# Conv taps at other rounds and in other homes, and a first step whose end is shared with GpSimd, in a convolution and GELU kernel

## The chip, the cores and the metric

One core of one Trainium2 chip. The metric is the device time of one execution in microseconds; the median of three runs stands for a kernel. Engines are named as the profile names them: PE (TensorE), ACT (ScalarE), DVE (VectorE), POOL (GpSimd), SP (SyncE, which only issues DMAs).

## What is computed

x has 8 x 4096 tokens of 192 features. Each feature group of 24 (8 heads) has 7 causal taps; the conv is a weighted sum of the last 7 tokens, with weights from a softmax. Its result goes through two matrix products with a GELU between them:

```python
w = softmax(weight)                       # (8 heads, 7 taps)
out = np.einsum('hk,bskhg->bshg', w, x_unf)   # depthwise causal conv
h = out.reshape(B * S, D) @ w_in          # 192 -> 2048
g = h * (1.0 / (1.0 + np.exp(-1.702 * h)))
return (g @ w_out)                        # 2048 -> 192
```

All of it is float32.

## The kernel before

**Tiles and steps.** The tokens are worked in 32 steps of 1024 (two batch halves n of 512 tokens, as 2 x 256 columns). Features lie on partitions, 64 of them at a time, in three chunks c. `w_in_s` holds 12 blocks of w_in and 9 places for sums of blocks; `conv_t` holds the conv result of one step in six own blocks (0 to 5) and their *common sums* (6 to 19: a sum or a difference of two blocks); each block lies there twice, the second time with its partition halves exchanged ("crossed"). `g` holds the GELU results. `slots` (three pairs of PSUM banks) and `sums` (one pair) are the accumulators.

**Step 0** (`first_step`) loads and rounds the weights while it computes, and does its second product in `second_first`, a generator that is stepped through between the stages. Its last part, up to L1020, forms in this order: the common sums of step 1 (`make_common_1`, L631: 9 sums on DVE, crossings on ACT by L603, one by SP's DMA), the late sums 16 to 19 (`make_late_1`), the sums of w_in (`sums_w_in`, 21 for column half v = 1, then 25 for v = 0, all on DVE, L435 to L443), the sums 13 to 15 (`make_rest_1`), and four transposes `turn` (L1025) that put the four quarters of the result into `osbs`, whence `store` (L1036) writes them out over SP's queue. The products of this part run through four half banks; the last one, `c21`, stays in a bank of `slots[1]` until its transpose has read it. Meanwhile `add_forms` (L480 on ACT, L482 on POOL) makes sums of w_out by copies and accumulating DMAs, and the first *taps* of step 2 are made. `load_x(3)` (L99, SP) is the last thing that `first_step` issues.

**Steps 1 to 31** have two halves. `hidden` runs the list `HIDDEN`, an order written out by hand: 41 *terms* (`mm`, L710; one product of a sum of w_in with a sum of the conv, in a Strassen-like scheme; the first is fetched at the end of the step before), copies of accumulators on ACT or DVE (`copy`, L801 and L803, into `KS`, the places k0 to k8), joins on DVE (L814), GELUs on ACT (L820, L827). `second` runs the list `PLAN` in the same way for the second product (L1107). Each term's operand pair (block of w_in, block of conv) stands in `TERMS[v][t]`; term `(0, 8)` of v = 0 is the first in `HIDDEN`, `(0, 14)`, which needs common sum 14, the nineteenth. `copy a k8`, which writes spot 1, stands ahead of the eighteenth, `join o2` and `gelu 0` near it. `HIDDEN` also holds `turn` (L518: transposes of x two steps on), `over`, `ve` and `vc` (common sums of the next step on POOL, and crossings on SP, L601).

**Taps.** The conv of the step after next is made in 21 taps (3 chunks x 7). In most of them ACT multiplies the shifted x by the weight of a tap (L567) into a *home*, some part of `g`, `osbs` or `room` that is free for a while (`TAP_SPOTS`, `TAP_HALVES`, `first_taps`; `spot(i)` names a place of 4 x 256 columns, spots 0 and 1 are `osbs`, where results wait for their store). The home is then added into `conv_t` by POOL (chunk 2, L569) or, pairwise in a tree, by accumulating DMAs of POOL's queue (`LATER`, L587; in steps up to 2 `TREE`, L592). `("tap",)` in the lists marks where one is made. Step 2 is an exception: chunks 0 and 2 by taps, chunk 1 by DVE, the tree of chunk 0 ending with `(3, 5)` and `(0, 3)`, which `end_taps` issues at the end of `first_step`.

**What orders the work.** Each engine's queue, SP's and POOL's too, runs in the order in which the program issues; waits come from the tiles that are read and written. A DMA's issue counts as an instruction of its queue and waits there for its operands.

Of the kernel before, what the change touches and what calls it, by code (L numbers as in the profile page):

```python
# [15 lines left out]
def kernel(  # L16
# [142 lines left out]
    TAP_HALVES = {1: ((1, 0), (1, 2), (11, 0), (2, 0), (2, 2), (11, 2)), 2: ((11, 2), (13, 0), (11, 2), (13, 2), (11, 2), (13, 0)), 3: ((12, 2), (16, 2), (15, 2), (16, 0), (15, 0), (12, 0))}  # L159
# [273 lines left out]
    def add_up(v, dst, a, op, b, eng=vec):  # L433
        if op == "+":
            eng.tensor_add(v(dst), v(a), v(b))  # L435
        elif op == "-":
            eng.tensor_sub(v(dst), v(a), v(b))  # L437
        elif op == "n":
            vec.scalar_tensor_tensor(
                out=v(dst), in0=v(a), scalar=-1.0, in1=v(b), op0=ALU.mult, op1=ALU.subtract  # L440
            )
        else:
            vec.tensor_scalar_mul(v(dst), v(a), -1.0)  # L443
# [81 lines left out]
    first_taps = [row(0, 6), row(0, 7)] + [spot(i)[:, k : k + 2, :] for i in (13, 18) for k in (0, 2)]  # L525
# [17 lines left out]
    def conv(big, c, k, ns=slice(0, 2), times=vec.tensor_scalar_mul):  # L543
# [99 lines left out]

    def make_rest_1():
        for item in SUMS_ES:
            sum_of(1, item, vec)
        for r in (V_S, V_E):
            if r[1] > r[0]:
                cross_run(1, *r, act.copy)
# [32 lines left out]
    def prepare(big):  # L682

        def convs(*cs):
            for c in cs:
                for k in range(K):
                    yield "", 0.76 if k else 0.48, lambda c=c, k=k: conv(big, c, k)

        if big < 3:
            yield from convs(1)  # L690
# [42 lines left out]
    def plain(u, m, n, v, slot, ks=range(NC), first=0):  # L733
# [40 lines left out]
    def hidden(big, tiles, work):  # L774
# [19 lines left out]
        def copy(eng, dst, src, sign):  # L794
# [4 lines left out]
            for out, i in pairs:  # L799
# [4 lines left out]
                else:  # L804
                    vec.tensor_scalar_mul(out, i, -1.0)

# [23 lines left out]

        def turn():
            if big + 2 < N_BIG:
                c = next(turns)
                if c == 0:
                    need(f"done {big + 1}")
                transpose_x(big + 2, c)
                if c == NC - 1 and big + 3 < N_BIG:
# [572 lines left out]
```

## Time and profile before

| | us |
|---|---|
| median of 3 runs (2325.21 to 2330.69) | 2327.47 |
| the profiled execution's own time | 2326.97 |
| its span, first to last instruction | 2325.2 |
| PE busy | 2291.7 |
| DVE, ACT, POOL busy | 2161.8, 1701.8, 1093.8 |

The granted TensorE clock is 0.994 on average. In rows of the timeline the first number is the start in us from the span's begin, the second the length, then engine, line, operation, tiles written and read, and the count of merged instructions; in brackets stands the idle time of the engine before them and what ended it. In rows of groups there stand the count, the busy time in us, the mean length in ns, and the idle time before with its releasers; in rows of DMA issues the count, the size and the median us from issue to landing. In a table of windows each engine's busy us are followed by the granted clock, the share of the DMA engines and GB/s. Matmul rows show fewer records than instructions in places; starts are reliable, ends are modelled.

### The profile page before, as it was taken

The numbers are of one execution on the slowest core, as the hardware profiler recorded it, in microseconds if no ns is written. First come the engines' busy times: TensorE is split into PE (matmuls) and PEld (weight loads), VectorE is DVE, ScalarE is ACT, GpSimd is POOL, SyncE is SP. The second block draws the span as 40 slices with busy tenths as digits, with TensorE's granted clock in tenths as the row PEclk, the third lists the DMA queues.
The fourth block names the chain that finished last, engine by engine and source line by source line (L and its number), as shares of the span: only waits on it lengthen the run. The fifth ranks groups of instructions, "written<-read, shape, count | busy, mean of one in ns | idle before, by whom it ended". The sixth has DMA issues, their size and how long they took to land.

```text
span 2325.2 us, 64148 instructions
## 1 busy us (share of the span) xinstructions
PE 2291.7 (99%) x25090; PEld 1321.8 (57%) x25090; DVE 2161.8 (93%) x3059; ACT 1701.8 (73%) x3338; POOL 1093.8 (47%) x1218
## 2 busy tenths in 40 slices
PE   9899999999999999999999999999999999999999
PEld 5265555555555755555655555555555555555555
DVE  8899999999999998999899899999999999999998
ACT  8677777777777777777677677777777777777745
POOL 1444554444554445544455444555444554454610
PEclk9899999999999999999999999999999999999999
DMA  9967789777797777987788877889877889776743
GB/s 202 155 126 153 152 167 177 152 153 155 144 180 156 153 151 149 174 166 147 141 158 167 165 154 153 159 154 176 161 155 151 159 163 175 156 153 132 150 98 69
DMA packets 347917, 358.12 MB, mean 154 GB/s; under 512 B 131424, under 2 KB 268896, under 8 KB 347616
## 3 DMA queue, kind: packets, MB, share of 16 engines
q0 software_dynamic: 82192, 196.32, 48.2%
q1 hardware_dynamic: 263776, 157.32, 29.8%
q8 instruction: 199, 3.26, 0.6%
q14 instruction: 102, 0.84, 0.1%
q10 hardware_dynamic: 1648, 0.39, 0.1%
HBM read 53.15 MB, written 25.17 MB: 34 GB/s over the span
## 4 chain that ended last, share of the span: by engine, by line
PE 88%; DVE 6%; DMA 2%; issue 2%; ACT 1%; POOL 1%; SPq 0%; DVEq 0%; ACTq 0%; POOLq 0%
PE slot L710 35%; PE slot L1107 26%; PE sums L1107 15%; PE sums L710 12%; DVE room L435 1%; DVE g L437 1%; DVE room L437 1%; DMA g<-in_moe_w_in_dram 0%; DMA room<-g 0%; DMA g<-osbs 0%; DVE osbs L1025 0%; DMA conv_t<-conv_t 0%; SPq L340 0%; POOL g L437 0%; DVE w_out_s L420 0%
## 5 line engine op out<-in xcount | busy, mean ns | idle before, releaser
L710 PE MATMUL slot<-conv_t,w_in_s 64*128 64x512 f32 x3372 | 931.3, 594 | 9.7 <-DVE osbs L1025 6.6
L1107 PE MATMUL slot<-g,w_form 128*32 128x256 f32 x5872 | 727.8, 380 | 0.1
L710 PEld LDWEIGHTS slot<-conv_t,w_in_s 64*128 64x128 f32 x3372 | 441.7, 188 | 342.5 <-issue 266.1
L437 DVE TENSOR_TENSOR g<-g 128x1024 f32<-128x1024 f32 x372 | 445.8, 1225 | 16.6 <-ACT g L827 9.2
L1107 PEld LDWEIGHTS slot<-g,w_form 128*32 128x32 f32 x5872 | 367.7, 110 | 121.4 <-ACT room L1132 11.6
L1107 PE MATMUL sums<-g,w_form 128*32 128x256 f32 x3800 | 427.6, 379 | 0.0
L710 PE MATMUL sums<-conv_t,w_in_s 64*128 64x512 f32 x1284 | 425.5, 593 | 0.3 <-DVE w_in_s L420 0.3
L437 POOL TENSOR_TENSOR conv_t<-conv_t 128x256 f32<-128x256 f32 x300 | 267.1, 963 | 223.6 <-PE slot L710 82.5
L820 ACT ACTIVATE g<-slot 128x512 f32<-128x512 f32 x494 | 265.1, 626 | 127.7 <-PE slot L710 127.2
L567 ACT ACTIVATE g<-xt,cw 128x512 f32<-128x512 f32 x418 | 289.6, 726 | 71.4 <-DVE g L437 44.7
L1107 PE MATMUL slot<-g,w_out_s 128*32 128x256 f32 x4080 | 324.0, 381 | 4.0 <-DVE room L435 3.8
L1083 POOL DMA_DIRECT2D g<-g x124 | 118.3, 954 | 436.7 <-PE slot L1107 236.8
L569 POOL TENSOR_TENSOR conv_t<-conv_t,g 128x512 f32<-128x512 f32 x180 | 293.7, 1632 | 52.1 <-ACT g L567 49.5
L1132 ACT COPY room<-slot 32x256 f32<-32x256 f32 x434 | 158.2, 365 | 202.0 <-PE slot L1107 189.4
L1107 PEld LDWEIGHTS sums<-g,w_form 128*32 128x32 f32 x3800 | 219.2, 110 | 79.5 <-ACT room L1132 5.7
L710 PEld LDWEIGHTS sums<-conv_t,w_in_s 64*128 64x128 f32 x1284 | 179.2, 187 | 123.9 <-issue 99.7
L1107 PEld LDWEIGHTS slot<-g,w_out_s 128*32 128x32 f32 x4080 | 162.8, 110 | 92.0 <-ACT g L820 11.4
L710 PE MATMUL slot<-g,w_in_s 64*128 64x512 f32 x556 | 205.2, 596 | 6.9 <-ACT room L801 6.5
L827 ACT ACTIVATE g<-g 128x1024 f32<-128x1024 f32 x155 | 170.9, 1102 | 0.4 <-DVE g L814 0.4
L1132 ACT COPY room<-sums 32x256 f32<-32x256 f32 x217 | 79.0, 364 | 94.0 <-PE sums L1107 83.1
L1107 PE MATMUL slot<-osbs,w_form 128*32 128x256 f32 x1240 | 147.2, 381 | 0.4 <-ACT slot L1136 0.3
L820 ACT ACTIVATE g<-sums 128x512 f32<-128x512 f32 x188 | 104.0, 616 | 58.7 <-PE sums L710 56.8
(241 smaller groups left out, 4029.3 us busy)
## 6 DMA issues: line engine op xcount, KB each, us to landing
g<-g POOLq DMA_DIRECT2D x124, 512.0 KB, 6.6
xin<-in_x_dram SPq DMA_DIRECT2D x240, 180.0 KB, 6.4
conv_t<-conv_t SPq DMA_DIRECT2D x662, 64.0 KB, 2.0
g<-g POOLq DMA_DIRECT2D x120, 256.0 KB, 6.4
out_dram<-osbs SPq DMA_DIRECT2D x186, 128.0 KB, 4.5
conv_t<-g POOLq DMA_DIRECT2D x89, 256.0 KB, 4.4
g<-g SPq DMA_DIRECT2D x248, 64.0 KB, 3.9
g<-room POOLq DMA_DIRECT2D x31, 512.0 KB, 5.5
```

The costliest lines, as they stand in the source:

```text
L435: eng.tensor_add(v(dst), v(a), v(b))
L437: eng.tensor_sub(v(dst), v(a), v(b))
L567: act.mul(home, conv_src(big, c, k), cw[:, c, k : k + 1])
L569: nc.gpsimd.tensor_add(dst, dst, home)
L710: nc.tensor.matmul(slot[h], w_in_s[halves[h], a, v * P : (v + 1) * P], src, start=first, stop=True, skip_group_check=True,)
L820: act.activation(dst[:, :, h, :], ot(bank(src, h)), AF.Gelu_apprx_sigmoid, scale=float(sign))
L827: act.activation(dst.rearrange("p o h t -> p h o t"), src, AF.Gelu_apprx_sigmoid, scale=float(sign))
L1083: nc.gpsimd.dma_start(out=spot(dst), in_=spot(a), accum_op=ALU.add)
L1107: nc.tensor.matmul(dst, w, t, start=first, stop=last, skip_group_check=True)
L1132: act.copy(to, d)
```

## The change

In the regular steps: one of the two taps at the start of `HIDDEN` goes, one is added near the end of `PLAN`, one near its start is added and a later one taken out (the first three taps come one place earlier); `TAP_HALVES` gives other homes to chunks 1 and 2, and two entries of `LATER` name other partners.

At step 0's end: the nine common sums and the 25 sums of w_in's half 0 go to POOL, the first ahead of everything else that POOL does from there on; an `n` sum is two instructions there. The crossings of 6 to 11 go from ACT to SP. Sum 13 is made by DVE before the last products, sums 14 and 15 by POOL behind ten taps (before: eight), with their crossing on SP. Two transposes of the result come between the last products; `c21` is copied by ACT to a place `last` in `room`, and the two other transposes and both stores move into step 1, behind the first two `copy v` (two parts). In step 1 the other taps, the convs of chunk 1, `turn`, `over`, `ve` and `vc` come later, by a list `count`. `first_taps` and `TAP_HALVES[3]` name other homes for step 2's taps: spot 18, which is also k6, is no longer one; spots 5 and 6 are.

```diff
-    TAP_HALVES = {1: ((1, 0), (1, 2), (11, 0), (2, 0), (2, 2), (11, 2)), 2: ((11, 2), (13, 0), (11, 2), (13, 2), (11, 2), (13, 0)), 3: ((12, 2), (16, 2), (15, 2), (16, 0), (15, 0), (12, 0))}
+    TAP_HALVES = {1: ((3, 0), (1, 0), (11, 0), (2, 0), (2, 2), (11, 2)), 2: ((11, 2), (13, 0), (16, 2), (15, 2), (11, 2), (13, 0)), 3: ((5, 0), (6, 0), (12, 2), (16, 2), (15, 2), (16, 0))}
...
+        elif op == "n" and eng is not vec:
+            eng.tensor_add(v(dst), v(a), v(b))
+            eng.tensor_scalar_mul(v(dst), v(dst), -1.0)
...
-    def sums_w_in(v):
+    def sums_w_in(v, eng=vec):
         for item in SUMS_W[v]:
-            add_up(lambda j: w_in_s[:, j, v * P : (v + 1) * P], *item)
+            add_up(lambda j: w_in_s[:, j, v * P : (v + 1) * P], *item, eng=eng)
...
-    first_taps = [row(0, 6), row(0, 7)] + [spot(i)[:, k : k + 2, :] for i in (13, 18) for k in (0, 2)]
+    first_taps = [
+        h if isinstance(h, int) else spot(h[0])[:, h[1] : h[1] + 2, :] for h in ((5, 2), 6, (13, 0), 7, (6, 2), (13, 2))
+    ]
+    first_taps = [row(0, h) if isinstance(h, int) else h for h in first_taps]
...
-        (1, 2): [(1, 1, 2)], (1, 4): [(1, 3, 4)], (1, 6): [(1, 5, 6)], (0, 0): [(1, 0, 1)], (0, 2): [(0, 1, 2)],
+        (1, 2): [(1, 2, 1)], (1, 4): [(1, 3, 4)], (1, 6): [(1, 5, 6)], (0, 0): [(1, 0, 2)], (0, 2): [(0, 1, 2)],
...
     def make_common_1():
         for item in SUMS_F + SUMS_B_1:
-            sum_of(1, item, vec)
-        for r in RAW_RUNS + [FIRST] + runs(*V_B):
-            cross_run(1, *r, None if r[1] - r[0] == 1 else act.copy)
+            sum_of(1, item)
+        for r in RAW_RUNS:
+            cross_run(1, *r, act.copy)
+        for r in [FIRST] + runs(*V_B):
+            cross_run(1, *r)
...
     HIDDEN = [
-        ("mm", 0, 8, 1, 1), ("tap",), ("tap",), ("mm", 0, 0, 2, 1), ("copy", "a", "k0", "p1", 1), ("mm", 0, 2, 3, 1),
+        ("mm", 0, 8, 1, 1), ("tap",), ("mm", 0, 0, 2, 1), ("copy", "a", "k0", "p1", 1), ("mm", 0, 2, 3, 1),
...
         def copy(eng, dst, src, sign):
...
+            if eng == "v" and after_copy:
+                after_copy.pop(0)()
...
         def tap():
-            next_tap()
             if big == 1:
+                convs_next(1)
+            if big > 1 or count.pop(0):
                 next_tap()
-                work(1.6, 2)
...
+        waiting, count = [], [0, 1, 1, 0, 1, 1] if big == 1 else []
...
         make_common_1()
+        sums_w_in(1 - FETCH[0], nc.gpsimd)
         sub(t2[1], b21[1], t2[1])
         sub(t2[0], b21[0], t2[0])
         make_late_1()
...
-        for v in (FETCH[0], 1 - FETCH[0]):
-            sums_w_in(v)
+        sums_w_in(FETCH[0])
+        sum_of(1, SUMS_ES[0], vec)
         next_tap()
         next_tap()
         steps = listed(a22, t2, (1, 0))
         for i in range(0, len(steps), 2):
             go(c21, steps[i : i + 2], first=False)
-            next_tap()
-            if i < 4:
+            for _ in range((3, 3, 2, 0)[i // 2]):
                 next_tap()
+            if i == 2:
+                turn(0, 0, blocks(p1), js)
+                cross_run(1, V_E[0], V_E[0] + 1)
+                turn(1, 1, blocks(p5), js)
+                convs_next(2)
         assert not side
         fetch()
-        turn(0, 0, blocks(p1), js)
-        make_rest_1()
-        turn(1, 1, blocks(p5), js)
+        act.copy(last, whole(c21))
+        convs_next(1)
+        for item in SUMS_ES[1:]:
+            sum_of(1, item)
+        cross_run(1, V_E[0] + 1, V_S[1])
         add(q12, q12, whole(c12))
-        turn(1, 0, blocks(whole(c21)), js)
-        store(0, 0)
-        turn(0, 1, blocks(q12), js)
-        store(0, 1)
+
+        def out(m, n, src):
+            turn(m, n, blocks(src), js)
+            store(0, n)
+
+        after_copy.append(lambda: out(0, 1, q12))
+        after_copy.append(lambda: out(1, 0, last))
...
     PLAN = [
...
-        ("turn", 1, 0, 0, "k6"), ("store", 0, 0), ("main", 24, 19, "p5", 0), ("go", 2),
+        ("turn", 1, 0, 0, "k6"), ("store", 0, 0), ("main", 24, 19, "p5", 0), ("go", 1), ("tap",), ("go", 1),
```

More of the change, by code (lines that the diff above doesn't have):

```diff
@@ L642, in make_late_1 @@
             cross_spot(b)
[L644 to L649, printed above, removed]
     pieces = []
@@ L682, in prepare @@
     def prepare(big):
[L684 to L687, printed above, removed]
         if big < 3:
-            yield from convs(1)
+            for k in range(K):
+                yield "", 0.76 if k else 0.48, lambda k=k: conv(big, 1, k)
         yield f"conv {big}", 0.0, lambda: None
@@ L829, in gelu, with next_turn @@
             )
-        def turn():
[L832 to L837, printed above, removed]
-                    load_x(big + 3)
+        def next_turn():
+            c = next(turns)
+            if c == 0:
+                need(f"done {big + 1}")
+            transpose_x(big + 2, c)
+            if c == NC - 1 and big + 3 < N_BIG:
+                load_x(big + 3)
+        def turn():
+            if big + 2 < N_BIG and (not count or count.pop(0)):
+                next_turn()
+            if len(count) < 2:
+                count.clear()
+                while waiting:
+                    waiting.pop(0)()
         def tap():
-            next_tap()
             if big == 1:
+                convs_next(1)
+            if big > 1 or count.pop(0):
                 next_tap()
-                work(1.6, 2)
         def early(i):
@@ L913, in second_first @@
         p5, q12 = (flat_room[0:n3, 2 * t4 + i * TOK : 2 * t4 + (i + 1) * TOK] for i in range(2))
-        p1 = room0[0:n3, 3 * w4 : 3 * w4 + TOK]
+        p1 = room0[0:n3, 2 * w4 : 2 * w4 + TOK]
+        last = room[0:n3, ROOMS[2], 0:TOK]
         assert 3 * w4 + TOK <= (2 * NV_ES + NV_F) * T and 3 * w4 <= NR * T and NV_B == NR
```

51 lines of the change are left out of this document (34 added, 17 removed), and 8 rows, old and new, of the table PLAN.

## The prediction

> **What bounds the kernel now.** The page's first table says where the time is not: of a span of 2325.2 us TensorE is busy for all but about 33.
>
> ```profile
> PE 2291.7 (99%) x25090; PEld 1321.8 (57%) x25090; DVE 2161.8 (93%) x3059; ACT 1701.8 (73%) x3338; POOL 1093.8 (47%) x1218
> ```
>
> So a change can win little in the 30 regular steps and something only where PE stands. The timeline of PE alone, read for its bracketed idle times, finds that place, the start of step 1; the table by windows adds the clock.
>
> ```profile
> 92.90 1.06 PE L710 MATMUL sums<-conv_t,w_in_s 64*128 64x512 f32 x4
> 93.79 1.02 PE L710 MATMUL slot<-conv_t,w_in_s 64*128 64x512 f32 x2
> 101.36 3.77 PE L710 MATMUL slot<-conv_t,w_in_s 64*128 64x512 f32 x6 [6.55 <-DVE osbs L1025]
> 106.62 2.56 PE L710 MATMUL sums<-g,w_in_s 64*128 64x512 f32 x4 [1.49 <-ACT room L801]
> 115.10 1.19 PE L710 MATMUL slot<-conv_t,w_in_s 64*128 64x512 f32 x3 [2.51 <-ACT g L801]
> ```
>
> ```profile
> 95.00:100.00 5.00, 0.00 (x0) 0.00 (x0) 4.90 (x18) 0.47 (x2) 0.74 (x1) 0.91 0.59 93
> 100.00:105.00 5.00, 3.64 (x6) 1.17 (x6) 4.89 (x9) 4.92 (x10) 2.58 (x5) 0.50 0.52 101
> ```
>
> PE idles 10.6 us in three waits, and behind the first the granted clock is 0.50. What step 1 loses in all comes from step starts (the first term, `(0, 8)`):
>
> ```profile
> 183.09 1.13 PE L710 MATMUL slot<-conv_t,w_in_s 64*128 64x512 f32 x4
> ```
>
> ```profile
> 326.99 1.13 PE L710 MATMUL slot<-conv_t,w_in_s 64*128 64x512 f32 x4
> ```
>
> ```profile
> 397.54 1.13 PE L710 MATMUL sums<-conv_t,w_in_s 64*128 64x512 f32 x4
> ```
>
> A clean step takes 397.54 - 326.99 = 70.55 us; step 1 takes 183.09 - 92.90 = 90.2, so 19.6 us lie there. A term takes 93.79 - 92.90 = 0.89. The 18th term, which matters below, stands 17 x 0.89 = 15.1 after the first, hence 55.4 before the next step: measured back from 183.09, at **127.7**.
>
> **What the change takes away.** The 6.55 ends when VectorE has turned `c21` out of PSUM; VectorE is late because of its chain of sums:
>
> ```profile
> 97.67 0.22 DVE L443 TENSOR_SCALAR w_in_s<-w_in_s 128x128 f32<-128x128 f32 x1
> ...
> 101.23 0.67 DVE L1025 STREAM_TRANSPOSE osbs<-room 96x512 f32<-96x512 f32 x1
> ```
>
> After it, `act.copy(last, c21)` frees the bank as soon as the product ends near 92, and the 9 common sums and the 25 sums of w_in's half 0 leave VectorE. The 1.49 goes with the four ACT taps ahead of the first copies. The third is a copy to `k6`, spot 18:
>
> ```profile
> 104.60 2.27 POOL L592 DMA_DIRECT2D g<-g  x1
> ...
> 114.68 0.86 POOL L592 DMA_DIRECT2D conv_t<-g  x1 [7.81 <-DMA g<-g]
> ```
>
> The tap DMA issued at 104.60 reads spot 18, and both POOL's next issue and ACT's copy wait for its landing. With spot 18 no longer a home the 2.51 goes too. So all three waits lose their cause, up to 19.6 us. What is late next decides.
>
> **What is late next: one chain over GpSimd and SP.** POOL and SP run their queues in program order. Rows for the prices:
>
> ```profile
> 56.93 0.86 POOL L592 DMA_DIRECT2D w_form<-w_form  x1 [2.11 <-DMA w_form<-w_form]
> 61.12 0.86 POOL L592 DMA_DIRECT2D conv_t<-w_form  x1 [3.34 <-DMA w_form<-w_form]
> ```
>
> ```profile
> 72.56 4.75 POOL L482 DMA_DIRECT2D w_form<-w_out_s  x5
> ...
> 88.61 3.39 POOL L592 DMA_DIRECT2D g<-g  x3
> 94.54 1.20 POOL L592 DMA_DIRECT2D conv_t<-g  x1 [2.54 <-PE sums L710]
> ```
>
> ```profile
> L437 POOL TENSOR_TENSOR conv_t<-conv_t 128x256 f32<-128x256 f32 x300 | 267.1, 963 | 223.6 <-PE slot L710 82.5 <-PE sums L710 56.5 <-DMA conv_t<-conv_t 50.3
> ```
>
> ```profile
> L369 POOL TENSOR_TENSOR room<-osbs 128x64 f32<-128x64 f32 x1 | 0.3, 308 | 0.0
> ```
>
> ```profile
> 115.24 9.33 POOL L569 TENSOR_TENSOR conv_t<-conv_t,g 128x512 f32<-128x512 f32 x6
> ```
>
> 1. POOL is free of `add_forms(1)` at 72.56 + 4.75 = 77.3. Nine common sums at 0.963 end at 86.0.
> 2. 28 instructions (25 sums, three of them in two parts) of 128x128 follow. No row has this size on POOL: it lies between 0.308 (64 columns) and 0.963 (256), so their end E lies between 94.6 and 113. Linear between the two it is 0.53, and E = **100.7**. I take that. (Term 8 needs the 23rd sum, there at 99.8, and would start at 99.1: no wait to speak of.)
> 3. Queued behind: `add_forms(2)`. Its third DMA needs the first one landed: 61.12 - 56.93 = 4.2 between two such issues. With an issue each 0.5, the first tap DMA goes at E + 5.3, and `(0, 1)`, which needs it landed, 94.54 - 88.61 = 5.9 later, E + 11.2.
> 4. Two tap adds of 9.33 / 6 = 1.56 and the sums 14 and 15 of 0.963 end at E + 16.8 = 117.5. So term 19, `(0, 14)`, has no operand before about 120, and `gelu 0`, which overwrites homes of those taps, is held on ACT until 115.5.
> 5. SP waits there too: `cross_run(1, 14, 16)` needs sum 15, and behind it stand `load_x(3)` and then the two stores, which the change moves from ahead of `load_x(3)` into step 1.
>
> ```profile
> 101.33 4.04 SPq L1036 DMA_DIRECT2D out_dram<-osbs  x6
> 105.42 9.50 SPq L99 DMA_DIRECT2D xin<-in_x_dram  x8
> ```
>
> ```profile
> 140.56 4.04 SPq L99 DMA_DIRECT2D xin<-in_x_dram  x8
> ```
>
> ```profile
> xin<-in_x_dram SPq DMA_DIRECT2D x8, 180.0 KB, 7.3
> ```
>
> ```profile
> out_dram<-osbs SPq DMA_DIRECT2D x6, 128.0 KB, 2.7
> ```
>
> Two crossings (1.1), the loads (9.5 beside POOL's DMAs, 4.04 in a quiet stretch; POOL issues five DMAs then, so 9.5), two more store issues (1.3) and a landing of 2.7 put `store(0, 1)` in DRAM at E + 31.4 = 132.1; behind the loads' own landing of 7.3 it would be E + 34.7. ACT's copy to `k8` overwrites spot 1, which that store reads, and term 18 waits for the copy: 0.5 more, **132.6**. Meanwhile `join o2` on VectorE waits as long: its rows hold home `(6, 2)`, which the tap DMA `(3, 5)` reads, issued at about E + 19 and 114.68 - 104.60 = 10.1 from its landing.
>
> Sum for step 1: term 18 at 132.6, not 127.7, is 4.9; PE comes back at the low clock after a long gap, some 5 us at 0.50 as in the window row, 2.5 more: **+7.4**. Without the chain it would be -19.6.
>
> **The regular steps.** One tap leaves the start of the hidden list for the end of the plan. There ACT waits for POOL's add on home `(11, 2)`, and behind the taps stands the first copy out of PSUM, for which PE waits:
>
> ```profile
> 186.03 1.34 ACT L567 ACTIVATE g<-xt,cw 128x512 f32<-128x512 f32 x2 [2.47 <-POOL conv_t L569]
> ```
>
> ```profile
> 322.66 1.20 POOL L587 DMA_DIRECT2D g<-g  x1
> ```
>
> ```profile
> g<-g POOLq DMA_DIRECT2D x1, 256.0 KB, 6.1
> ```
>
> and the same DMA in a later step:
>
> ```profile
> g<-g POOLq DMA_DIRECT2D x1, 256.0 KB, 5.2
> ```
>
> ```profile
> 327.70 1.34 ACT L567 ACTIVATE g<-xt,cw 128x512 f32<-128x512 f32 x2 [0.25 <-POOL conv_t L569]
> ```
>
> Now the copies start at 327.70 + 1.34 = 329.05. After the change the one tap left writes `(15, 2)`, which the DMA issued at 322.66 still reads until 322.66 + 6.1 = 328.8: tap 0.7, copies at 329.4, 0.35 later than now; by the landing of 5.2 they start at 328.5, but no term wants them before about 329. The wait changes its releaser and hardly its length, and in the few starts like 183 it stays, because that DMA is late with the rest. Bounds -7 (the 0.25 of the row of 327.70 gone at 29 starts) and +10 (0.35 x 29); between the two landings I take -1. The tap's new place near the plan's end costs ACT 0.7 among 0.4 us copies with idle time between them; if that cover is gone it is the same 0.7 a step, inside the bound. The first three taps come one place earlier, `(3, 0)` gives them a free home: nothing.
>
> **The edits that I cost at nothing** hold as long as their cover does. The crossings of sums 6 to 11 go from ACT to SP's queue:
>
> ```profile
> 77.08 6.73 ACT L603 COPY conv_t<-conv_t 64x768 f32<-64x768 f32 x8
> ```
>
> ACT wins half of these 6.73 and spends 1.3 of it on two more taps (0.67 each, by the row of 186.03) ahead of the copy of `c21`, which ends near 94, where the second term wants the bank. SP's crossings wait for POOL: the run 6 to 8 for its fifth sum, 77.3 + 5 x 0.96 = 82.1, and with the slowest landing quoted here, 7.3, it is there at 89.4, before the first term at 92.9; the run 9 to 11 is there at 93.3 for the fifth term at 96.5. VectorE's sums 16 and 17 wait for POOL's sums 6 and 7 until 81.2, about as long as its own two subtractions of `t2` last. Were a cover gone, PE would wait some us before term 18 and lose nothing more, since that term is late by itself. The convs of c = 1, `end_forms`, and step 3's turns and `load_x(4)` move back within step 1, over engines that idle while PE waits.
>
> So 2326.97 of the profiled execution + 7.4 - 1 = 2333.4; the median of the three runs lies 0.5 above that execution: **2334**.
>
> **Rivals.**
> - *The chain is short (faster).* Place: SP's queue ahead of `store(0, 1)`. If the loads go at 4.04, the store lands at E + 25.9, and it turns into a gain when term 18 with its low clock is ready before 127.7, that is E below 98.8. With E = 95.5 step 1 gains 3.3, and if the waits at the starts go as well (-7): about 2317. For it: E may be 94.6, and a start like 183 costs PE what ACT waits there. Against: five accumulating DMAs run beside the loads.
> - *It cancels*: E near 97 and loads between the two prices; 2327.
> - *The two engines lock each other (slower still).* VectorE's 21 sums of half 1 run beside POOL's. The rows:
>
> ```profile
> 178.43 0.42 DVE L435 TENSOR_TENSOR room<-room 96x256 f32<-96x256 f32 x1
> ```
>
> ```profile
> 322.33 1.00 DVE L435 TENSOR_TENSOR room<-room 96x256 f32<-96x256 f32 x1
> ```
>
> ```profile
> 606.57 4.18 DVE L437 TENSOR_TENSOR room<-room 96x256 f32<-96x256 f32 x1
> ```
>
> The same add takes 0.42 with POOL on DMA, 1.00 beside a POOL sum, and the 4.18 runs beside two POOL sums and two tap adds. One sum waiting for the other makes the two lists run one after the other. 21 sums of some 0.22 (the row of 97.67) are 4.6 more for E, and VectorE reaches `add(q12, ...)` some 11 us later, so that PE stands at the third term already; term 18 still waits for SP, 4.6 later: 2338, with landings behind the loads 2342. The Trainium skill ("SBUF — State Buffer", Who interferes with whom) says just this: a VectorE instruction with two SBUF inputs and a GpSimd instruction that reads SBUF exclude each other for a whole instruction. By that rule, the three rows agree, the sharing wins no time at all for sums that overlap.
>
> **How the numbers follow.** Forecast (2329 to 2338) 0.40; locked 0.20; cancels 0.17; short chain 0.23. A measurement of this kernel tells 0.2%, about 4.7 us, from no change. Locked and nine tenths of the forecast are slower: 0.56; the cancelling case and the rest are the same: 0.21; faster 0.23. The range takes the late landing with some of the 0.35 a step above (2345) and most of the short chain below (2318).
>
> **What would show it.** Right: PE without a wait of 6 us near 95, then a long one ending between 125 and 137 whose copy is ACT's to `osbs` (L801), with `store(0, 1)` on SP behind eight loads; POOL's w_in sums ending near 101; POOL's tap DMAs after that; clock 0.50 behind the wait. Wrong: sums 14 and 15 done by 105, or SP's stores landing before 120, or starts of regular steps whose first copies come clearly earlier than 2 us.

## The result and the profile after

| | before | after |
|---|---|---|
| median, us | 2329.09 (10 runs, 2325.21 to 2332.01) | 2336.57 (10 runs, 2332.51 to 2339.84) |
| ratio | | 1.0034 [1.0024, 1.0044] |
| profiled execution, its span | 2326.97, 2325.2 | 2337.84, 2336.1 |
| first term of step 2, of the last step | 183.09, 2251.04 | 194.36, 2261.96 |

The changed kernel is slower by 0.34%; the forecast was 2334 (2318 to 2345). The last row of the table says where. PE's timeline of the kernel after, at the two step starts:

```profile
194.36 1.13 PE L707 MATMUL slot<-conv_t,w_in_s 64*128 64x512 f32 x4
```

```profile
2261.96 1.13 PE L707 MATMUL sums<-conv_t,w_in_s 64*128 64x512 f32 x4
```

and the last start of the kernel before:

```profile
2251.04 0.70 PE L710 MATMUL sums<-conv_t,w_in_s 64*128 64x512 f32 x2
```

Up to step 2 the new kernel loses 11.3 us. The 29 steps from there to the last start take 2067.95 before and 2067.60 after, and what follows is equal (74.2 in both). So the two profiled executions differ in step 1, but for 0.4 us: its first term starts at 92.90 before and at 93.28 after. They stand 10.9 apart, the medians 7.5: the profiled run of before lies 2.1 below its median, that of after 1.3 above.

In the first table of the page after, GpSimd is busy 24 us longer than before and VectorE as long as before:

```profile
PE 2290.0 (98%) x25090; PEld 1331.0 (57%) x25090; DVE 2161.6 (93%) x3023; ACT 1703.4 (73%) x3331; POOL 1117.9 (48%) x1257
```

The windows up to step 2 and over the 29 steps take this apart. VectorE is busy 164.5 us before and 161.2 after up to step 2, where 34 sums left it and those that stayed got longer (the rows stand near the end). In the 29 steps it is busy 3.1 longer; e12 and e4 lie 2.1 and 3.5 below the kernel before there, so a few us are the spread of single profiles.

PE's timeline of the kernel after shows step 1, with the idle time ahead of a row in brackets:

```profile
93.28 1.02 PE L707 MATMUL sums<-conv_t,w_in_s 64*128 64x512 f32 x4
...
101.15 1.22 PE L707 MATMUL slot<-conv_t,w_in_s 64*128 64x512 f32 x1 [4.89 <-DVE room L1038]
...
118.35 2.04 PE L707 MATMUL slot<-conv_t,w_in_s 64*128 64x512 f32 x4 [1.17 <-ACT g L819]
136.24 4.01 PE L707 MATMUL sums<-conv_t,w_in_s 64*128 64x512 f32 x8 [15.85 <-ACT osbs L798]
```

The waits of 6.55, 1.49 and 2.51 are gone. In their place stand 4.89 at the third term and 15.85 at term 18. The third term's accumulator is free when VectorE has done `add(q12, ...)`, which reads it for a quarter of step 0's result (L1038). Term 18's is free when ACT has copied it to `k8`, that is to spot 1 of `osbs`, and the copy has to wait until `store(0, 1)` has read that spot. The reader follows this long wait back, first on ACT, then on SP; VectorE's `join o2` waits beside it, for the tap DMA `(3, 5)`:

```profile
117.70 1.09 ACT L819 ACTIVATE g<-slot 128x512 f32<-128x512 f32 x2 [6.16 <-POOL conv_t L575]
135.61 1.07 ACT L798 COPY osbs<-sums 128x512 f32<-128x512 f32 x2 [16.82 <-DMA out_dram<-osbs]
```

```profile
130.32 1.29 DVE L813 TENSOR_TENSOR g<-slot,room 128x512 f32<-128x512 f32 x2 [11.92 <-DMA g<-g]
```

```profile
97.92 22.26 SPq L607 DMA_DIRECT2D conv_t<-conv_t  x4
120.22 8.77 SPq L99 DMA_DIRECT2D xin<-in_x_dram  x8
129.09 5.38 SPq L1073 DMA_DIRECT2D out_dram<-osbs  x6
```

SP issues two of the four crossings at 97.92, stands until 119 for sum 15, then brings x for step 3, and only then stores. GpSimd's timeline says why sum 15 is late:

```profile
86.93 0.46 POOL L439 TENSOR_TENSOR w_in_s<-w_in_s 128x128 f32<-128x128 f32 x1
...
102.98 0.53 POOL L446 TENSOR_SCALAR w_in_s<-w_in_s 128x128 f32<-128x128 f32 x1
103.45 1.77 POOL L485 DMA_DIRECT2D w_form<-w_form  x2
...
108.78 3.70 POOL L598 DMA_DIRECT2D g<-g  x3
...
117.62 1.43 POOL L437 TENSOR_TENSOR conv_t<-conv_t 128x256 f32<-128x256 f32 x2
```

The w_in sums end at 103.5, the tap DMAs go at 108.8, and the last common sum ends at 119.0. In the table by windows (busy us and count of PE, PEld, DVE, ACT and POOL, then the granted clock, the share of the DMA engines and GB/s) the clock is 0.50 from the wait on until PE has run again:

```profile
125.00:130.00 5.00, 0.00 (x0) 0.00 (x0) 0.00 (x0) 0.00 (x0) 0.00 (x0) 0.50 1.14 257
130.00:135.00 5.00, 0.00 (x0) 0.00 (x0) 1.29 (x2) 0.00 (x0) 4.32 (x4) 0.50 1.22 237
135.00:140.00 5.00, 3.76 (x9) 3.16 (x11) 2.84 (x3) 3.97 (x6) 4.41 (x5) 0.51 0.41 89
```

No engine computes anything between 125 and 130: only the DMA engines work, and they are full.

### The profile page after: what moved, and what is told of

Read it like the earlier page. It is cut to its first block, busy times and chain, and to the rows that moved or that the text cites. A ratio compares the mean times of both kernels' runs of the same rounds, so it can differ in the third digit from the quotient of the medians.

```text
span 2336.1 us, 64199 instructions
## 1 busy us (share of the span) xinstructions
PE 2290.0 (98%) x25090; PEld 1331.0 (57%) x25090; DVE 2161.6 (93%) x3023; ACT 1703.4 (73%) x3331; POOL 1117.9 (48%) x1257
## 4 chain that ended last, share of the span: by engine, by line
PE 82%; DVE 6%; DMA 5%; POOL 3%; issue 2%; ACT 1%; SPq 1%; POOLq 0%; DVEq 0%; ACTq 0%
PE slot L707 33%; PE slot L1144 24%; PE sums L1144 13%; PE sums L707 12%; DVE g L437 1%; DMA osbs<-room 1%; DVE room L437 1%; POOL conv_t L437 1%; DVE room L435 1%; SPq L99 1%; DMA g<-in_moe_w_in_dram 1%; DMA xin<-in_x_dram 1%; DMA g<-g 1%; DMA w_form<-w_form 0%; DMA room<-g 0%
## 5 line engine op out<-in xcount | busy, mean ns | idle before, releaser
L437 POOL TENSOR_TENSOR conv_t<-conv_t 128x256 f32<-128x256 f32 x310 | 273.9, 957 | 220.1 <-PE slot L707 85.6
L1120 POOL DMA_DIRECT2D g<-g x124 | 118.3, 954 | 445.7 <-PE slot L1144 220.1
L593 POOL DMA_DIRECT2D g<-g x116 | 118.4, 1020 | 65.2 <-ACT g L573 58.1
```

What stands on the lines that cost most here:

```text
L593: nc.gpsimd.dma_start(out=out, in_=src, accum_op=ALU.add)
L1120: nc.gpsimd.dma_start(out=spot(dst), in_=spot(a), accum_op=ALU.add)
```

## The experiments

**Theory.** One chain sets step 1: GpSimd's sums (their end is the prediction's E), its tap DMAs, sums 14 and 15, SP's queue, `store(0, 1)`, ACT's copy to `k8`, term 18; beside it, nearly as late, the tap DMA `(3, 5)` for `join o2`. **Rivals.** The two engines lock each other, and what PE loses at the third term is the loss; or the moved tap of the regular steps carries it.

All twelve runs, each against the kernel before on the same chip. "Step 2" is the start of its first term in the profile, "29 steps" the time from there to the last start, "clean" the median of those steps:

| run | ratio | step 2 | 29 steps | clean |
|---|---|---|---|---|
| before | 1 | 183.09 | 2067.95 | 70.67 |
| after | 1.0034 [1.0024, 1.0044] | 194.36 | 2067.60 | 70.98 |
| e1 load behind the stores | 1.0043 [1.0028, 1.0058] | 194.19 | 2066.12 | 70.88 |
| e2 sums 14, 15 on VectorE, early | 1.0009 [0.9999, 1.0018] | 189.61 | 2061.99 | 70.86 |
| e3 e2 and tap DMA early | 0.9999 [0.9989, 1.0009] | 185.93 | 2064.46 | 71.12 |
| e4 step 0's part alone | 1.0037 [1.0024, 1.0050] | 195.81 | 2066.39 | 70.69 |
| e5 sums 14, 15 on VectorE | 1.0007 [0.9997, 1.0016] | 191.06 | 2061.51 | 70.90 |
| e6 e5 and tap DMA early | 0.9997 [0.9987, 1.0007] | 186.38 | 2062.46 | 70.94 |
| e7 e6 and half 0 in two parts | 0.9987 [0.9977, 0.9996] | 183.26 | 2062.86 | 70.75 |
| e8 e7, forms late, q12 early | 0.9993 [0.9984, 1.0003] | 177.49 | 2070.58 | 70.89 |
| e9 q12 early alone | 1.0042 [1.0027, 1.0057] | 195.58 | 2065.06 | 70.88 |
| e11 forms late alone | 1.0038 [1.0023, 1.0053] | 192.42 | 2066.73 | 70.87 |
| e12 sums unshared | 0.9970 [0.9958, 0.9983] | 178.40 | 2061.98 | 70.84 |
| e13 e12 and q12 early | 0.9958 [0.9943, 0.9973] | 180.61 | 2060.71 | 70.86 |

The 29 steps are the same program in all rows but before and e4, and yet spread over 2060.71 to 2070.58 in single profiles. A difference of a few us there says nothing; step 1 is read from the traces, the whole from the ratios. Where an experiment builds on another (e3 on e2, e6 on e5, e7 on e6), the intervals of the two overlap: the order that the traces show is not proved by those ratios.

### e1: the load behind the stores

```diff
         end_taps()
-        load_x(3)
...
         after_copy.append(lambda: out(1, 0, last))
+        after_copy.append(lambda: load_x(3))
```

> The changed kernel, with load_x(3) issued behind the two stores of step 0 instead of ahead of them. Theory (one chain over GpSimd and SP sets step 1): the three DMAs of store(0, 1) are issued at about 120.3 to 121.7 instead of 129.1 to 130.1 and land near 126; ACT's copy to k8 and term 18 come near 127 instead of 136.2. The other wait of the same place, join o2 on VectorE for the tap DMA that lands at 130.2, stays and is now the last: the term that needs join p0 starts near 132 instead of 139.8. So -7.5 us: 2329, ratio to the kernel before 1.000. Rival (the two engines lock each other, PE's loss is made at the third term and every later wait is only its echo): the 15.85 us wait gets another releaser and the time stays within 2 us of 2336.6.

Measured: no gain. SP, PE and VectorE in this kernel:

```profile
120.10 8.65 SPq L1074 DMA_DIRECT2D out_dram<-osbs  x6
128.80 6.26 SPq L99 DMA_DIRECT2D xin<-in_x_dram  x8
```

```profile
131.62 4.26 PE L707 MATMUL sums<-conv_t,w_in_s 64*128 64x512 f32 x8 [11.35 <-ACT osbs L798]
```

```profile
130.69 1.29 DVE L813 TENSOR_TENSOR g<-slot,room 128x512 f32<-128x512 f32 x2 [12.49 <-DMA g<-g]
...
140.53 0.78 DVE L521 STREAM_TRANSPOSE xt<-xin 128x576 f32<-128x576 f32 x1 [5.24 <-DMA xin<-in_x_dram]
```

The store was issued 9 us sooner and landed only 4.6 sooner: its third DMA took 8.6 to land (issued 122.29, landed 130.89) beside GpSimd's accumulating ones. Then VectorE stood 5.24 for the load, now the later one, ahead of a join that PE needs (PE stood 0.68 for it), and step 2 begins where it did. Of the 4.6 us won at term 18, 1.6 are left at the start of the second product (157.49 for 159.07) and 0.2 at step 2; what took each part is not shown. The expectation of both theories fell: the long wait did shrink (against the rival), but SP's order was not what had to be mended. Two waits ended within 6 us of each other in the kernel after, and a third was made.

### e2, e3: sums 14 and 15 on VectorE, at an earlier place

```diff
-        sum_of(1, SUMS_ES[0], vec)
+        for item in SUMS_ES:
+            sum_of(1, item, vec)
...
-        for item in SUMS_ES[1:]:
-            sum_of(1, item)
```

e3 also has `end_taps(1)` ahead of `add_forms(3)`. At this place the sums overwrite rows that still hold a factor (`s4`) of the last side products to `q12`, so that block of step 0's output comes out wrong in e2 and e3, and only their times are of use. PE waits for the sums in the midst of step 0:

```profile
97.81 1.06 PE L964 MATMUL slot<-g,conv_t 128*32 128x512 f32 x1 [10.16 <-DVE conv_t L437]
```

> The changed kernel, with the common sums 14 and 15 back on VectorE, right behind sum 13. Theory (chain): SP's crossing of 14 and 15 goes near 99 instead of 119.1, the loads stand between 100 and 106, the stores near 107 and land by 112. The store is then out of the way, and the next to end is gelu 0 on ACT, which still waits for GpSimd's tap adds until 117.7: copy to k8 near 119, term 18 near 119.5. Then join o2 waits for the tap DMA (3, 5), issued near 120 without loads beside it and landed near 127 to 129: the term behind join p0 starts near 129.5 instead of 139.8. So -10: 2326.5, ratio 0.999. Rival (locked engines): two more sums on VectorE make add(q12, ...) 0.8 us later, PE stands at the third term 0.8 longer, nothing else changes: 2337.

> As the one with sums 14 and 15 on VectorE, and the tap DMA (3, 5) issued ahead of add_forms(3), right behind the two tap adds. Theory (chain): the DMA goes near 117.6 and lands near 123.4, join o2 follows at once, and the term behind join p0 starts near 125.5 instead of 139.8; term 18 near 119.5. So -14: 2322.5, ratio 0.997. Rival (locked engines): no change against the one before it, 2337. A third possibility: add_forms(3), now later, holds step 1's second product instead, which would show as a wait of PE after 145.

Expected 0.999 and 0.997, measured 1.0009 and 0.9999. Even with 10 us more of waiting in step 0 both are faster than the changed kernel. That says that the 15.85 covered whatever came ahead of it, the third term's 4.89 among it; the rival had asked for 2337.

### e5, e6: the same, behind the last use of those rows

```diff
         for item in SUMS_ES[1:]:
-            sum_of(1, item)
+            sum_of(1, item, vec)
```

and in e6 alone, ahead of the DMAs of `add_forms(3)`:

```diff
+        end_taps(1)
         add_forms(3)
         end_taps()
```

> The changed kernel, with the common sums 14 and 15 on VectorE at the place where GpSimd had them in the program (behind the last step of c21). Theory (chain): SP's crossing of 14 and 15 goes near 101.5 instead of 119.1, the loads stand between 102 and 107, the stores go near 107 to 109 beside the three tap DMAs and land by 118. Then gelu 0 holds ACT until 117.7 as now, and term 18 starts near 119.5 instead of 136.2; join o2 waits for the tap DMA (3, 5), issued near 120 and landed near 127 to 129, and the term behind join p0 starts near 129.5 instead of 139.8. So -10: 2326.5, ratio 0.999. Rival (locked engines): add(q12, ...) comes 0.8 us later, PE stands at the third term 0.8 longer, nothing else changes: 2337.

> As the one with sums 14 and 15 on VectorE behind the loop, and the tap DMA (3, 5) issued ahead of add_forms(3). Theory (chain): that DMA goes near 118 and lands near 123.5, the term behind join p0 starts near 125.5 instead of 139.8: -14, 2322.5, ratio 0.997. Rival (what holds PE is the number of bytes that the DMA engines move in this stretch, not the order of the queues): the landings stretch to the same end, -10 at the most.

Measured 1.0007 for 0.999, and 0.9997 for 0.997: the right order, about six tenths of the step that each was to make from 1.0034. PE in e5:

```profile
101.75 1.22 PE L707 MATMUL slot<-conv_t,w_in_s 64*128 64x512 f32 x1 [6.10 <-DVE room L1038]
119.99 3.84 PE L707 MATMUL slot<-g,w_in_s 64*128 64x512 f32 x4 [4.51 <-DVE g L813]
134.00 7.26 PE L707 MATMUL slot<-conv_t,w_in_s 64*128 64x512 f32 x15 [4.05 <-DVE slot L813]
```

The wait of 15.85 is gone. Part of the gain is missing because GpSimd's own DMAs are later: the load is now issued from 102 to 107 and the stores behind it, beside the four DMAs of `add_forms(2)`, which land 4.9 to 7.1 us after their issue instead of 3.0 to 3.6, and the tap DMAs stand behind those. GpSimd's timeline of e5, against 114.17 in the kernel after for the same DMA `(0, 1)`:

```profile
119.43 0.86 POOL L598 DMA_DIRECT2D conv_t<-g  x1 [3.81 <-DMA g<-g]
```

So `(0, 1)`, the tap adds and `gelu 0` all come 5 us later. e6 then takes `join o2` out of the way (its tap DMA is issued at 123.44 and landed at 126.79) and step 2 begins 4.7 sooner than in e5.

### e7, e8: GpSimd's list in two parts, and its forms later

e7 is e6 with this:

```diff
-        sums_w_in(1 - FETCH[0], nc.gpsimd)
+        sums_w_in(1 - FETCH[0], nc.gpsimd, slice(0, 12))
...
-        add_forms(2)
...
+            if i == 0:
+                sums_w_in(1 - FETCH[0], nc.gpsimd, slice(12, None))
...
+        add_forms(2)
         end_taps(1)
```

(and the third and fourth sum of `add_forms(2)` moved to `add_forms(3)`).

> As the one before, and GpSimd's 25 sums of w_in's half 0 in two parts (12 and 13 items) with the first two tap DMAs between them, and add_forms(2) behind the tap adds instead of ahead of the tap DMAs. Theory (chain, its length set by E and by what stands between E and the tap adds): the tap DMA (0, 1) goes near 106 instead of 114.2, the tap adds end near 109.5 instead of 117.6, gelu 0 no longer holds ACT, the tap DMA (3, 5) goes near 111 and lands near 117, and PE runs on from the third term without a wait of over 2 us: the term behind join p0 near 121.6. So -18: 2318.5, ratio 0.9955. Rival (the DMA engines are the limit in this stretch): stores, loads and tap DMAs now meet between 105 and 120, land 3 to 6 us later, and the gain stops near that of the kernel before it, 2322.

Measured 0.9987 for 0.9955. The first tap adds came forward as expected, and term 18 waits for nothing. VectorE's sums still run beside GpSimd's here and are still long (0.454 us each, by the group that stands near the end for the kernel after with 0.482): the loss went without the sharing being undone, when what stood behind GpSimd's list came sooner. The next wait was GpSimd's again, as PE and POOL of e7 show:

```profile
131.08 7.94 PE L707 MATMUL slot<-conv_t,w_in_s 64*128 64x512 f32 x20 [5.12 <-ACT g L819]
```

```profile
124.11 6.29 POOL L575 TENSOR_TENSOR conv_t<-conv_t,g 128x512 f32<-128x512 f32 x4
```

A gelu writes the homes that these four adds still read, and the adds stand behind the DMAs of `add_forms`. e8 takes in e9's edit (below) and puts those DMAs behind the adds, in `vl` of step 1, where `form_sums` issues the DMAs of a stage that `add_forms` then leaves out:

```diff
                 next_tap()
                 next_tap()
                 convs_next(1)
+                form_sums(2)
+                form_sums(3)
+                end_taps()
```

> The kernel with half 0 in two parts, and two edits more: add(q12, ...) ahead of the convs, and the DMAs of add_forms(2) and (3) with the tap DMA (0, 3) behind the four tap adds of step 1's hidden list instead of ahead of them. Theory (chain): the third term starts near 99 instead of 100.8 and its wait is 2 us shorter; the four tap adds stand between 111 and 117.5 instead of 124.1 and 130.4, so the wait of 5.1 for the gelu behind them (131.1) goes: together -6 or -7 against that kernel, 2317, ratio 0.996. Rival (the edits meet the next wait of the same length: the tap DMA (3, 5) or the store lands later than 120, because seven more DMAs are moved at the same time): -2 at the most.

In step 1 this is right: step 2 begins at 177.49, 5.8 sooner than in e7. But the time did not follow: 0.9993, where 0.996 was expected. In e8's profile step 2 itself takes 75.12 and two later steps 74.85 and 75.48. The start of step 2, on PE and on ACT:

```profile
182.79 1.13 PE L712 MATMUL slot<-g,w_in_s 64*128 64x512 f32 x3 [2.28 <-ACT room L803]
```

```profile
178.23 0.72 ACT L578 ACTIVATE g<-xt,cw 128x512 f32<-128x512 f32 x1 [1.72 <-DMA g<-g]
...
181.36 0.72 ACT L578 ACTIVATE g<-xt,cw 128x512 f32<-128x512 f32 x1 [2.02 <-DMA g<-g]
```

The one tap left at a step's start (181.36) waits for the DMA that reads its home, the wait that the prediction weighs for regular steps, and PE waits for the copy behind it. The tap that the change put near the plan's end (178.23) waits for a DMA too, which the prediction did not count. What decides in which steps these waits come is open.

### e9: q12 early, alone

```diff
-                convs_next(2)
...
+        add(q12, q12, whole(c12))
         act.copy(last, whole(c21))
-        convs_next(1)
+        convs_next(3)
...
-        add(q12, q12, whole(c12))
```

> The changed kernel with add(q12, ...) on VectorE ahead of the three convs instead of behind two of them: nothing else. It takes about 2 us from the third term's wait of 4.9 (98.9 instead of 101.2 for its start). Theory (chain): the wait at term 18 grows by as much, the time stays within 1 us of 2336.6, ratio 1.0035. Rival (locked engines: what PE loses at the third term is the loss): -2, and the wait at term 18 keeps its length.

PE in e9:

```profile
99.31 0.69 PE L707 MATMUL slot<-conv_t,w_in_s 64*128 64x512 f32 x1 [2.88 <-DVE room L1032]
...
135.00 4.26 PE L707 MATMUL sums<-conv_t,w_in_s 64*128 64x512 f32 x8 [15.91 <-ACT osbs L798]
```

The third term's wait fell by 2 us, the one at term 18 stayed, and the ratio is 1.0042: no gain. Term 18 came 1.2 sooner, yet step 2 began 1.2 later. So the third term was not what the time hung on, against the rival; that the long wait would grow by as much, as the theory had it, is not what the row shows either.

### e4: step 0's part alone

From step 2 on, `HIDDEN`, `PLAN`, the homes and `LATER` are those of the kernel before:

```diff
-        for item in HIDDEN:
+        for item in HIDDEN if big == 1 else HIDDEN_R:
```

> Only the part of the change at the end of step 0 and in step 1's hidden list: from step 2 on, the tap's places, the homes and the LATER sums are those of the kernel before. Theory (chain; the regular steps sum to nothing): step 1 keeps its wait ending near 136, the steps 2 to 30 sum to 2068 as in both kernels, 2336.6, ratio 1.003; the clean steps are back at 70.55 to 70.7 and the long starts of 73 to 77 come back in five or so places. Rival (the moved tap carries a loss in the regular steps, and step 1 less than it seems): the time falls to 2330 to 2333.

The ratio stays at 1.0037, and step 1 keeps its wait:

```profile
136.92 4.26 PE L709 MATMUL sums<-conv_t,w_in_s 64*128 64x512 f32 x8 [15.49 <-ACT osbs L828]
```

So the loss is step 0's part, and the regular part is worth nothing that these runs can tell. It does do something. The groups of ACT's taps into `g` between 185 and 2250 us, before and after (after, six taps of step 1 fall into this window):

```profile
L567 ACT ACTIVATE g<-xt,cw 128x512 f32<-128x512 f32 x396 | 274.9, 726 | 68.9 <-DVE g L437 43.4 <-POOL conv_t L569 17.9 <-DMA room<-g 4.5
```

```profile
L573 ACT ACTIVATE g<-xt,cw 128x512 f32<-128x512 f32 x402 | 282.3, 727 | 80.4 <-DVE g L437 43.4 <-DMA g<-g 33.0 <-DMA room<-g 0.4
```

The wait for GpSimd's add (17.9) became a wait for the tap DMA (33.0). A clean step is 70.67 and 70.69 with the old taps (before, e4) and 70.75 to 71.12 with the new ones (the other twelve). In this pair the long steps make up for it: the five above 72 add 18.2 us over 70.67 before, and 11.0 over 70.98 after. In the other profiles those above 72 add 16.4 with the old taps (e4) and 4.2 to 15.4 with the new ones.

### e11: what slows the loads and the store

```diff
                 next_tap()
                 next_tap()
                 convs_next(1)
+                form_sums(3)
```

(in `vl` of step 1; `add_forms(3)` at the end of step 0 keeps only its copies on ACT)

> The changed kernel with only the four DMAs of add_forms(3) moved behind step 1's taps, out of the stretch from 119 to 129; SP's queue keeps its order. It asks why the loads of load_x(3) take 8.8 us to issue and the store 5.4 to land. If it is the accumulating DMAs of GpSimd beside them (bytes in flight): the loads issue in 5 to 6, the store lands near 130 instead of 135.5 and the tap DMA (3, 5), issued at 119, near 126; term 18 near 130.5, so -6: 2330.5, ratio 1.001. If it is the loads themselves: term 18 stays at 136 and the time at 2336.6.

On ACT and VectorE of e11 both waits end sooner, at 132.30 and 123.16 instead of 135.61 and 130.32:

```profile
132.30 1.07 ACT L803 COPY osbs<-sums 128x512 f32<-128x512 f32 x2 [14.08 <-DMA out_dram<-osbs]
```

```profile
123.16 1.29 DVE L818 TENSOR_TENSOR g<-slot,room 128x512 f32<-128x512 f32 x2 [5.36 <-DMA g<-g]
```

The loads now take 5.5 us to issue (119.64 to 125.11) instead of 8.8, and the tap DMA `(3, 5)` lands in 4.6 instead of 9.1: what slowed them was the four DMAs beside them. The two prices of the prediction for the loads, 9.5 beside GpSimd's DMAs and 4.04 in a quiet stretch, are the two ends of this. The store still took 5.1 to land, behind the loads. Of 3.3 us won at term 18, 1.9 arrive at step 2, and the ratio (1.0038, where 1.001 was expected) does not tell that from nothing.

### e12: the sums back on VectorE

```diff
         for item in SUMS_F + SUMS_B_1:
-            sum_of(1, item)
+            sum_of(1, item, vec)
...
-        sums_w_in(1 - FETCH[0], nc.gpsimd)
...
-        sums_w_in(FETCH[0])
+        for v in (FETCH[0], 1 - FETCH[0]):
+            sums_w_in(v)
```

> The changed kernel with the nine common sums and the 25 sums of half 0 back on VectorE in the order of the kernel before (half 1 first); everything else of the change stays, the copy of c21 by ACT and the late stores too. Theory (E, the end of GpSimd's sums, heads the chain): GpSimd issues the tap DMAs near 95 as in the kernel before, SP's crossing of 14 and 15 goes near 104, the store lands near 114, and none of them is last any more. VectorE comes to add(q12, ...) some 4 us later, so PE stands at the third term until about 105 instead of 101.2; from there 15 terms and the low clock put term 18 near 121 instead of 136.2 and 127.7 (before's equivalent): -15 against the changed kernel, 2321.5, ratio 0.997. Rival (the sharing is what the change wins, and the loss lies in the moved stores): the third term waits for VectorE, the stores are held by SP as now, and the time stays above 2335.

Measured 0.9970, as expected, and faster than both kernels. PE, GpSimd and SP of e12:

```profile
104.65 1.22 PE L707 MATMUL slot<-conv_t,w_in_s 64*128 64x512 f32 x1 [8.88 <-DVE room L1038]
...
121.08 2.47 PE L707 MATMUL sums<-conv_t,w_in_s 64*128 64x512 f32 x8
```

```profile
92.14 3.66 POOL L598 DMA_DIRECT2D g<-g  x3
...
101.25 2.21 POOL L437 TENSOR_TENSOR conv_t<-conv_t 128x256 f32<-128x256 f32 x2
```

```profile
100.80 3.77 SPq L607 DMA_DIRECT2D conv_t<-conv_t  x4
104.62 8.68 SPq L99 DMA_DIRECT2D xin<-in_x_dram  x8
113.40 6.11 SPq L1073 DMA_DIRECT2D out_dram<-osbs  x6
```

GpSimd's tap DMAs go 16.6 us sooner than after (92.14 against 108.78), SP's queue passes 15.6 sooner. VectorE is done with `add(q12, ...)` 3.5 later (104.59 against 101.09), which PE sees as a wait of 8.88 instead of 4.89. Term 18 starts at 121.08, where the forecast for this run was 121. The store landed at 120.35 and not at 114, since the loads again took 8.7 beside GpSimd's DMAs, so it ends just as PE gets there: the same queue in the same order as in the kernel after, only begun earlier. It is the head of the chain, GpSimd's list, that made that kernel slow.

### e13: q12 early where nothing covers it

e12 with e9's edit, and the three convs behind step 1's third VectorE copy.

> The kernel with the sums back on VectorE, and the order of add(q12, ...) changed in it: VectorE does it right behind the loop, and the three convs that stood ahead of it and behind it follow the third VectorE copy of step 1. In the changed kernel the same third-term wait was covered by the one at term 18, and shortening it gave nothing. Here nothing covers it. Theory: the third term starts near 102 instead of 104.65, VectorE's copies follow at once, term 18 near 119 unless the store (landed 120.35) becomes the last: then 120.5. So -1 to -2.5 against that kernel: ratio to the kernel before 0.996. Rival (VectorE is full from 105 to 125, so the convs are only put off and joins come later by as much): no change, ratio 0.997, with a wait of PE for VectorE between 110 and 125.

```profile
99.99 1.22 PE L707 MATMUL slot<-conv_t,w_in_s 64*128 64x512 f32 x1 [4.40 <-DVE room L1032]
...
121.77 2.87 PE L707 MATMUL sums<-conv_t,w_in_s 64*128 64x512 f32 x7 [1.59 <-ACT osbs L798]
```

The third term is 4.7 sooner, and term 18 is not: it waits for the store again. The ratio, 0.9958, is what was expected (0.996), but its interval overlaps e12's, and by the trace step 2 begins 2.2 later than in e12 (180.61), so a gain is not shown. SP's queue is the bound of this stretch even with the sums on VectorE.

## Why the prediction was right

- **The place and the sign.** All three waits of before lost their cause, and one chain took their place, ending in ACT's copy behind `store(0, 1)`. The signs that the prediction named are there: no wait of 6 us near 95 (4.89 instead), the copy to `osbs` (L801 of before is L798 now), the store behind eight loads, the clock of 0.50; the sums of w_in ended at 103.5, not near 101. e12 shows the head of the chain: with those sums off GpSimd, term 18 comes at 121.08 and the kernel is faster than before.
- **E, mis-sized by 2.8.** Taken at 100.7, measured 103.5. The prediction had no row of the size of the w_in sums and took the straight line between two others. The nine common sums took 10.0 us instead of 8.7 (the first two took 1.56 and 2.67, beside VectorE's long subtraction at 77.48), the 28 instructions of half 0 took 16.6, 0.59 each for the 0.53 of the straight line; GpSimd began 0.3 sooner than summed.
- **From E to the store in DRAM, nearly as summed**: 31.4 expected, 32.0 measured (135.51 for the third of its DMAs). Errors cancel, which is luck: sum 15 came 1.3 sooner than by the rows, the issues of SP took 0.9 less, and the landing took 5.4 instead of 2.7 (the DMA engines were full, by the windows). E + 34.7, the other end, was not reached.
- **Term 18** at 136.24 instead of 132.6; from there to step 2 58.1 for 55.4 + 2.5. So up to step 2 the profile lost 11.3 against a forecast of 7.4. The medians (+7.5 against a forecast of +6.4) hide this: the profiled pair and the medians differ by 3.4. That the median comes within 1.1 of the forecast is luck in part.
- **The regular steps**: -1 expected, -0.35 between the profiles. The prediction had the mechanism (the releaser changes from GpSimd's add to the tap DMA), but not that a clean step grows by 0.3 while the long ones shrink in this pair. By e4 the sum can't be told from nothing.
- **The third term** had no wait in the sum: the prediction took `add(q12, ...)` into account only in a rival. PE did stand there, 4.89, which cost nothing that the runs show, because the wait at term 18 covered it (e2, e9).
- **The rival of the locked engines** had named that wait, and the engines do slow each other, but the two lists did not run one after the other. (Of the rival's three rows, the short one of 0.42 runs while GpSimd stands idle, not on a DMA; its argument is the same.) The groups of VectorE's sums of half 1 in the kernel after, and of both halves in e12, where GpSimd does none:

```profile
L435 DVE TENSOR_TENSOR w_in_s<-w_in_s 128x128 f32<-128x128 f32 x10 | 4.4, 482 | 0.0
```

```profile
L435 DVE TENSOR_TENSOR w_in_s<-w_in_s 128x128 f32<-128x128 f32 x21 | 5.4, 286 | 0.2
```

  and of GpSimd's in the kernel after, about the time of those sums (86.9 to 97.5) and behind them (from 97.5 on):

```profile
L435 POOL TENSOR_TENSOR w_in_s<-w_in_s 128x128 f32<-128x128 f32 x9 | 4.6, 518 | 0.2
```

```profile
L435 POOL TENSOR_TENSOR w_in_s<-w_in_s 128x128 f32<-128x128 f32 x3 | 2.3, 761 | 0.1
```

  Beside each other VectorE's sums grow from 0.286 to 0.482, while GpSimd's take 0.518, about what the straight line gave. So the 4.6 more for E that this rival had priced did not come from there. GpSimd lost later: the last group's mean is 0.761, beside VectorE's transposes, convs and `add(q12, ...)`, and one sum there takes 1.29 (at 100.77).
- **The short chain** would have needed E below 98.8, and the cancelling case E near 97. It was 103.5.

One line that the prediction shows is not the one meant: the transpose that ended the wait of 6.55 is VectorE's at 100.61, which reads `c21` (`osbs<-slot`); the row at 101.23 is the next one. Nothing hangs on the 0.6.

Where the win of e12 over the kernel before comes from is argued, not shown by a run of its own. In the two profiles e12 leads by 4.7 at step 2 and by 10.7 at the end; the other 6.0 lie in the 29 steps, where single profiles differ by as much, so how much of the win is step 1's is open. In step 1, e12's wait for VectorE (8.88, at the third term) is longer than the old one (6.55, at the second), but from there to term 18 it takes 16.4, where before took 26.1 (101.36 to 127.49), with one term more in it. That stretch held the four ACT taps ahead of the copies and the copy to `k6` behind the tap DMA, and the new homes and taps took these away.

## What to carry to other kernels

Before work is shared out to an idle engine, write down what is queued behind it on that engine and on the queues that wait for it: here the sharing let VectorE come to `add(q12, ...)` 3.5 us sooner and put off GpSimd's tap DMAs by 16.6 us (after against e12), and GpSimd's list headed the chain to the next step. A long wait covers the ones ahead of it, so test a suspected wait only where nothing covers it, and expect the next one within a few us (e1, e7, e13). A transfer's price goes with what else is in flight: take it from a row with the same neighbours, or both ends.

## What the runs showed of the hardware

- The same 256 KB tap DMA landed 9.1 us after its issue with GpSimd's four accumulating DMAs issued just ahead of it and the loads beside it (the kernel after), and 4.6 after with the loads but without those four (e11). The two issue rows, of the kernel after and of e11 (KB, median us to landing):

```profile
g<-g POOLq DMA_DIRECT2D x1, 256.0 KB, 9.1
```

```profile
g<-g POOLq DMA_DIRECT2D x1, 256.0 KB, 4.6
```

- SP's issue of eight loads took 5.5 us without those four DMAs (e11) and 8.8 beside them (after), so the store behind it on SP started later too.
- Where small sums ran on VectorE and GpSimd side by side, VectorE paid most: 0.482 us for a sum instead of 0.286, while GpSimd's took 0.518, with 0.46 as the shortest (no run has its list undisturbed). VectorE's 21 sums took 8.3 us with some 16 of GpSimd's instructions beside them (88.67 to 96.94, after) and 4.9 without (e12); 16 times 0.46 is 7.4, so one after the other would be about 12.2 (an estimate; the profile's spans of GpSimd are rough). The Trainium skill ("SBUF — State Buffer", Who interferes with whom) has a VectorE instruction with two SBUF inputs contend with a GpSimd instruction that reads SBUF; the rows agree that they contend. If they excluded each other for whole instructions, as the prediction's rival had it, the two lists would have needed those 12.2; the measured 8.3 decides, and says that in this stretch they did not.
